# The prologue of an attention-plus-SwiGLU block on one core: the first token tile in two halves over two queues, its turned copy in two moves, and a shorter clear

## The chip, the cores and the metric

The kernel runs on one core of one Trainium2 chip. The time is that of one execution in microseconds (us); lower is better. Three runs of the kernel before gave 557.51, 557.83 and 559.01 us; the median is 557.83 us.

## What is computed

There are 2048 tokens of width 576. They are normalised (layernorm without gain or bias) and go through windowed causal attention (32 heads of width 18, window 256). A SwiGLU network with inner width 4608 runs on the same normalised tokens. The result is the sum of the tokens, the attention output and the network's output:

```
x = A_x
xn = _layernorm(x, axis=-1)
return x + _A_ref(xn, A_wqkv, A_wo) + _B_ref(xn, B_w1, B_w3, B_w2)
```

`_A_ref` projects to q, k and v, forms masked scores, takes a softmax, multiplies with v and projects with wo; `_B_ref` is `(silu(xn @ w1) * (xn @ w3)) @ w2`. All inputs are bf16.

## The kernel before

**Chunks.** The tokens go through in four chunks of 512 (loop at L959), each of four tiles of 128 tokens. A chunk has projections (`proj_part`, matmuls at L461), 36 SwiGLU units (matmuls at L713) with the attention scores woven in between (L587), and a second phase (L785) that multiplies with w2 and wo. Everything before L959 is the **prologue** of chunk 0: it loads the first four token tiles, normalises and turns them, and runs chunk 0's projections.

**How order and waits come about.** The program is a list of operations that is written out by hand. `add` (L59) appends an operation to its engine with the names of the buffers it reads (`r`), writes (`w`) or adds to (`j`); `resolve` (L90) turns these names into semaphore waits. Each engine runs its operations strictly in list order. A buffer name written once has one group of writers; every reader waits for all of them. DMAs are issued by SyncE (queue SPq) and by ScalarE (queue ACTq), in the order of their lists.

**The prologue in order.** The line numbers are those that the profile uses.

- L810 is ScalarE's table load and a small square root; L811 to L812 load the token tiles: tile 0 on SPq, tile 3 on ACTq, tile 1 on SPq, tile 2 on ACTq (`load_x`, DMA at L298, 128 rows of 576 elements each, into `xp`).
- L814 loads the first 512 rows of the v weights on SPq in two parts (`wv0`, `wv1`), L818 the last 64 rows on ACTq, once for each half of the partitions (`wvd`). L835 and L839 load the q and k weights on SPq.
- L821 clears `oq` on VectorE (256 f32 columns; later a buffer of the attention output). The cleared tile is the operand of **warming matmuls** (`warm`, L827): ten of 512 columns ahead of the first real work and one of 512 and one of 256 columns after the first turn. Their results are not used.
- Statistics: VectorE's `bn_stats` at L357 and L359 and `bn_aggr` at L360 for each tile. Tile 0 then gets its root on ScalarE (L362), a reciprocal (L382) and its normalised form `xn` (L386) with a small copy on GpSimd (L389). Tiles 1 and 2 get theirs through GpSimd (L365, L367) and VectorE (L371, L374). Tile 3 gets its sums on ScalarE (L860), a root (L876), a reciprocal (L882) and also L371 and L374.
- `xn_turn` (L399): ten transposes on TensorE (L406), five column blocks by two row halves, into two PSUM banks; then one move by ScalarE (L413) of 128x640 elements to `xnT`, the operand of all later matmuls.
- `proj_part` (L438) makes the matmuls of a projection in two parts: part 0 has ten (n from 0 to 4 by two row halves), part 1 has eight. For a v projection of tile i, matmul n reads column block n of `xnT` of that tile and the weights `wv0` (n of 0, 1), `wv1` (2, 3) or `wvd` (4).

TensorE's list in the prologue is: ten warming matmuls; turn of tile 0; two warming matmuls; v of tile 0, part 0; turn of tile 1; v of tile 0, part 1; turn of tile 2; v of tile 1, part 0; turn of tile 3; and then the rest of the projections. ScalarE's list is: root of tile 0; the sum over tile 3; the move of tile 0's turned copy; the sum of squares over tile 3; its root; the moves of tiles 1, 2 and 3.

Of the kernel before, what the change touches and what calls it, by code (L numbers as in the profile page):

```python
# [5 lines left out]
dt = mybir.dt  # L6
ACT = mybir.ActivationFunctionType
# [37 lines left out]
class _Prog:  # L45
# [13 lines left out]
    def add(self, eng, fn, r=(), w=(), j=(), dma=None, after=()):  # L59
        deps = []  # L60
        for k in r:
            deps += self.bufs[k].writers
        for k in w:
            g = self.bufs.get(k)
            if g is not None:
                deps += g.ahead(eng)
        for k in j:
            g = self.bufs[k].before
            if g is not None:
                deps += g.ahead(eng)  # L70
        op = _Op(eng, fn, deps + list(after), dma)
        op.after = tuple(after)
        self.n[eng] += 1
        op.pos = self.n[eng]
        if dma is not None:
            self.dma_count[dma] = self.dma_count.get(dma, 0) + 16
            op.cnt = self.dma_count[dma]
        for k in r:
            self.bufs[k].readers.append(op)
        for k in w:  # L80
            self.bufs[k] = _Gen([op], self.bufs.get(k))
        for k in j:
# [82 lines left out]
def bass_parallel_sum__sliding_block__glu_gated_swiglu__prompt_kernel(  # L165
# [17 lines left out]
    CH = 512  # L183
    NC = S // CH
    TB = CH // 128
# [7 lines left out]
    x2 = A_x[0]  # L193
    out2 = out[0]
    P = _Prog(nc)
    add = P.add

    with ExitStack() as es:

        def sb(name, shape, dtype=dt.bfloat16):  # L200
            return es.enter_context(nc.sbuf_tensor(name, shape, dtype))
# [4 lines left out]
        xp = [sb(f"xp{i}", [128, D]) for i in range(NXP)]  # L206
# [74 lines left out]
        def half_bank(b):  # L281
            return PS[:, b, :].bitcast(dt.bfloat16)
# [9 lines left out]
        xp_ctr = 0  # L292
# [106 lines left out]
        def xn_turn(t, banks, eng="dve"):  # L399
            i = t % 2  # L400
            c, tt = divmod(t, TB)
            for k in range(5):
                for r in range(2):
                    r0 = 64 * r
                    bv = half_bank(banks[r])[:, 64 * k:64 * k + 64]
                    add("pe", lambda e, bv=bv, r0=r0, k=k: e.transpose(  # L406
                        bv, xn[i][r0:r0 + 64, k * 128:(k + 1) * 128], ident[r0:r0 + 64, r0:r0 + 64],
                        tile_position=(r0, 0)),
                        r=[("xn", i), "ident"] + ([("xnd", i)] if k == 4 else []), **{"j" if k else "w": [("ps", banks[r])]})
            both = PS[:, banks[0]:banks[0] + 2, :].bitcast(dt.bfloat16)  # L410
            src = both[:, :, 0:320].rearrange("p r (k f) -> p k r f", f=64)
            dst = xnT[:, c % 2, :, tt * 128:(tt + 1) * 128].rearrange("p k (r f) -> p k r f", f=64)
            move = (lambda e: e.tensor_copy(dst, src)) if eng == "dve" else (lambda e: e.activation(dst, src, ACT.Copy))  # L413
            add(eng, move, r=[("ps", b) for b in banks], w=[("xnT", c % 2, tt)])

        def xn_send(t):
            i = t % 2
# [10 lines left out]
                    r=xk(c), dma=f"xnS{n}", **{"j" if n else "w": ["xnS"]})  # L428

        def xk(c):  # L430
            return [("xnT", c % 2, tt) for tt in range(TB)]


        def pair_of(c, i):

            return (((0, 1), (2, 3), (8, 4), (5, 6)) if c == 0 else ((8, 0), (1, 2), (3, 4), (5, 6)))[i]

        def proj_part(c, what, banks, part, behind=()):  # L438

            kind, i = what  # L440
            last = []
            for n in range(5 - part):
                for r in range(2):
                    x = r ^ part
                    kd, r0 = (4 if n == 4 else n), 64 * r
                    rows = slice(r0, r0 + 64)
                    out_ = PS[:, banks[x], :]
                    if kind == "q":
                        t = pair_of(c, i)[x]
                        st, mv = wp[rows, kd, t, :], xnT[rows, c % 2, kd, :]  # L450
                        keys = ["wpr" if n == 4 else "wp0"] + (["wp1"] if t > 3 else []) + (["wp8"] if t == 8 else []) + xk(c)
                    elif kind == "8":
                        out_ = PS[:, banks[x], 0:CH // 2]
                        st, mv = wp[rows, kd, i, :], xnT[rows, c % 2, kd, x * (CH // 2):(x + 1) * (CH // 2)]
                        keys = ["wpr", "wp0", "wp1"] + xk(c)
                    else:
                        out_ = PS[:, banks[x], 0:HD]
                        st, mv = xnT[rows, c % 2, kd, i * 128:(i + 1) * 128], wv[rows, kd, x * HD:(x + 1) * HD]
                        keys = ["wvd" if n == 4 else f"wv{n // 2}", ("xnT", c % 2, i)]
                    first = part == 0 and n == 0  # L460
                    op = add("pe", lambda e, out_=out_, st=st, mv=mv, n=n, r0=r0, first=first: e.matmul(  # L461
                        out_, st, mv, start=first, stop=(part == 1 and n == 3), tile_position=(r0, 0)),
                        r=keys, after=behind if n == 0 else (), **{"w" if first else "j": [("ps", banks[x])]})
                    if n == 4:
                        last.append(op)
            return last
# [188 lines left out]
        def o_scale(i):  # L655
            u3 = uqs[i].rearrange("p (n d) -> p n d", d=32)
            o3 = oq[:, :].rearrange("p (n d) -> p n d", d=32)[:, :, 0:Dh]
            add("dve", lambda e: e.reciprocal(rden[:], u3[:, :, Dh]), r=uq_keys[i], w=["rden"])
            add("pool", lambda e: e.tensor_tensor(  # L659
                o3, u3[:, :, 0:Dh], rden[:].unsqueeze(2).to_broadcast([128, CH // 32, Dh]), ALU.mult),  # L660
                r=uq_keys[i] + ["rden", "oq0"], w=["oq"])

        def o_turn(g, half):
            i = g // 2 % NOD
            c0 = half * (CH // 2)
            add("dve", lambda e: e.transpose(od[i][:, g % 2, c0:c0 + CH // 2], oq[:, c0:c0 + CH // 2]),  # L666
                r=["oq", "oq0"], **{"j" if half or g % 2 else "w": [("od", i)]})
# [140 lines left out]

        xslot = {}
        add("act", lambda e: e.activation(sm[:, 3:4], eps[:], ACT.Sqrt), r=["eps"], w=[("sm", 3)])  # L810
        for t in (0, 3, 1, 2):  # L811
            xslot[t] = load_x(t, "act" if t > 1 else "sp")  # L812
        for n in range(2):
            add("sp", lambda e, n=n: e.dma_start(  # L814
                wv[:, 2 * n:2 * n + 2, :], A_wqkv[256 * n:256 * n + 256, 2 * D:3 * D].rearrange("(kd p) f -> p kd f", p=128)),
                w=[f"wv{n}"], dma=f"wv{n}")
        for p in range(2):
            add("act", lambda e, p=p: e.dma_start(  # L818
                wv[64 * p:64 * p + 64, 4, p * HD:(p + 1) * HD], A_wqkv[512:576, 2 * D + p * HD:2 * D + (p + 1) * HD]),
                dma="wvd", **{"j" if p else "w": ["wvd"]})  # L820
        add("dve", lambda e: e.memset(oq[:].bitcast(dt.float32), 0.0), w=["oq0"])  # L821

        add("dve", lambda e: e.memset(qv[:, 0:2, :].bitcast(dt.float32), 0.0), w=[("q", g) for g in range(2)])

        def warm(b, *widths):
            for k, w in enumerate(widths):
                add("pe", lambda e, w=w: e.matmul(PS[:, b, 0:w], oq[:, 0:128], oq[:, 0:w], start=True, stop=True),  # L827
                    r=["oq0"], **{"j" if k else "w": [("ps", b)]})

        warm(4, *[CH] * 10)  # L830

        for h in range(2):
            for n in range(2):
                c0 = n * D + h * HD
                add("sp", lambda e, c0=c0: e.dma_start(  # L835
                    wa[:, 0:4, c0:c0 + HD], A_wqkv[0:512, c0:c0 + HD].rearrange("(kd p) f -> p kd f", p=128)),
                    dma=f"wqk{h}", **{"j" if n else "w": [f"wqk{h}"]})
# [32 lines left out]
        def turn(i):  # L870
# [6 lines left out]
            r=[("sm", 2), "eps"], w=[("sm", 3)])  # L877
# [23 lines left out]
        for h in range(2):  # L901
            a, b = 4 * h, 4 * h + 4
# [56 lines left out]
        for c in range(NC):  # L959
# [12 lines left out]
            start = 60 if c == 0 else 42  # L972
# [71 lines left out]
            for u in range(NF):  # L1044
# [7 lines left out]
                for n in range(9):  # L1052
                    into = nxt - (clock + 9 - n)
                    if (u, n) == JOINT[c]:
# [21 lines left out]
                        g = 2 * ja  # L1076
# [36 lines left out]
                if u in stat:  # L1113
                    t = (c + 1) * TB + stat[u]
# [4 lines left out]
                if u in apply:  # L1119
                    t = (c + 1) * TB + apply[u]  # L1120
# [6 lines left out]
                if c == 0 and u == 13:  # L1127
                    for t in range(4):
# [19 lines left out]
            banks = tail_bank = job()  # L1148
# [6 lines left out]
            for n, item in enumerate(p2_list(c)):  # L1155
# [20 lines left out]
                elif n in (100, 120) and c + 2 < NC:  # L1176
                    t = (c + 2) * TB + (n == 120)
# [32 lines left out]
```

## Time and profile before

| what | value |
|---|---|
| median of three runs | 557.83 us (557.51 to 559.01) |
| the profiled execution's own time | 557.61 us |
| its span, first to last instruction | 555.9 us |
| TensorE busy with matmuls | 552.1 us, 99% |
| VectorE, ScalarE, GpSimd busy | 56%, 47%, 29% |
| mean DMA rate | 155 GB/s |

All figures below are from this one profiled execution, whose time is 1.7 us longer than its span. A timeline row gives the start, the duration, the engine, the line, the operation and the tiles, and in brackets how long the engine had been idle before it and what ended that. PE is TensorE's matmuls and PEld its weight loads; the letter q after an engine's name marks its queue, that is, the issuing of a DMA. Matmuls overlap: one has a duration that includes its way through the array, while the next may start long before that ends.

### The profile page before, as it was taken

How to read it: one execution, taken by the hardware profiler on the slowest of the kernel's cores; microseconds unless marked ns; L12 is line 12 of the kernel's file. 1: busy time of each engine (PE TensorE's matmuls, PEld its weight loads, DVE VectorE, ACT ScalarE, POOL GpSimd, SP SyncE). 2: the span in 40 equal slices, each digit the busy share in tenths (PEclk: the TensorE clock that was granted, in tenths of full speed). 3: DMA queues.
4: the chain of work that ended last, by engine and by line, in shares of the span. 5: the costliest groups of instructions: out<-in, count | busy, mean ns of one | idle time of the engine just before them, and what ended most of it. 6: DMA issues, size and time to landing. Idle time of an engine off the chain costs nothing.

```text
span 555.9 us, 15754 instructions
## 1 busy us (share of the span) xinstructions
PE 552.1 (99%) x6772; PEld 346.6 (62%) x6772; DVE 311.4 (56%) x583; ACT 260.0 (47%) x359; POOL 162.7 (29%) x385
## 2 busy tenths in 40 slices
PE   8999999999999999999999999999999999999998
PEld 4666554677665545477766544847776554455776
DVE  6566978610365888851056687874105577678211
ACT  6457766100387774700048787550005777756000
POOL 5424534300034452530003454333001334333000
PEclk9999999999999999999999999999999999999999
DMA  9995989577377469756826748485582674553552
GB/s 244 201 206 139 211 188 243 106 196 186 90 143 164 114 138 167 217 136 174 203 57 140 169 126 198 123 205 136 151 187 54 138 174 122 150 151 82 142 150 65
DMA packets 127217, 85.96 MB, mean 155 GB/s; under 512 B 34452, under 2 KB 124908, under 8 KB 127148
## 3 DMA queue, kind: packets, MB, share of 16 engines
q1 hardware_dynamic: 125523, 83.49, 64.1%
q10 hardware_dynamic: 1624, 1.47, 1.0%
q8 instruction: 53, 0.87, 0.7%
q14 instruction: 17, 0.13, 0.1%
HBM read 71.29 MB, written 2.36 MB: 133 GB/s over the span
## 4 chain that ended last, share of the span: by engine, by line
PE 99%; ACT 0%; DVE 0%; issue 0%
PE ps L713 50%; PE ps L785 25%; PE ps L461 10%; PE ps L587 6%; PE ps L644 3%; PE ps L792 3%; PE ps L827 1%; PE ps L699 0%; PE ps L406 0%; ACT xnT L413 0%; DVE ofin L803 0%; DVE oq L821 0%
## 5 line engine op out<-in xcount | busy, mean ns | idle before, releaser
L713 PE MATMUL ps<-xnT,w 64*128 64x512 bf16 x1400 | 185.4, 376 | 0.0
L713 PE MATMUL ps<-xnS,w 64*128 64x512 bf16 x1120 | 154.0, 376 | 0.0
L785 PE MATMUL ps<-w,hT 128*128 128x288 bf16 x1156 | 146.7, 286 | 0.0
L728 DVE SCALAR_TENSOR_TENSOR gs<-th,ps 128x512 bf16<-128x512 bf16 x144 | 97.8, 679 | 76.6 <-ACT th L722 75.8
L785 PEld LDWEIGHTS ps<-w,hT 128*128 128x128 bf16 x1156 | 112.5, 98 | 28.9 <-issue 0.4
L713 PEld LDWEIGHTS ps<-xnT,w 64*128 64x128 bf16 x1400 | 73.0, 94 | 60.0 <-DVE ofin L653 0.2
L722 ACT ACTIVATE th<-ps 128x512 bf16<-128x512 f32 x144 | 85.6, 594 | 44.4 <-PE ps L713 42.0
L731 DVE SCALAR_TENSOR_TENSOR hT<-gs,ps 128x512 bf16<-128x512 bf16 x144 | 98.9, 687 | 4.9
L713 PEld LDWEIGHTS ps<-xnS,w 64*128 64x128 bf16 x1120 | 58.1, 94 | 46.7
L596 ACT ACTIVATE pt<-ps 128x1024 bf16<-128x1024 f32 (+1 forms) x70 | 70.8, 1011 | 31.2 <-PE ps L587 30.9
L474 ACT ACTIVATE stage<-ps 128x512 bf16<-128x512 f32 x16 | 9.5, 596 | 142.0 <-PE ps L461 142.0
L803 DVE TENSOR_TENSOR ofin<-ps,xp 128x288 bf16<-128x288 f32 x31 | 13.4, 455 | 108.3 <-PE ps L699 58.1
L623 POOL TENSOR_TENSOR hT<-hT,mk 128x128 int32<-128x128 int32 (+1 forms) x59 | 24.0, 429 | 170.5 <-ACT hT L596 170.3
L623 POOL TENSOR_TENSOR pt<-pt,mk 128x128 int32<-128x128 int32 (+1 forms) x124 | 49.9, 427 | 28.8 <-ACT pt L596 28.8
L587 PE MATMUL ps<-qv,kv 64*128 64x320 bf16 (+4 forms) x528 | 52.8, 260 | 0.0
L587 PEld LDWEIGHTS ps<-qv,kv 64*128 64x128 bf16 x528 | 27.4, 94 | 26.2 <-ACT hT L596 1.5
L596 ACT ACTIVATE w<-ps 128x1024 bf16<-128x1024 f32 (+1 forms) x32 | 32.3, 1010 | 12.3 <-PE ps L587 12.2
L461 PE MATMUL ps<-xnT,wp 64*128 64x512 bf16 (+1 forms) x360 | 38.0, 355 | 0.0
L596 ACT ACTIVATE hT<-ps 128x1024 bf16<-128x1024 f32 (+1 forms) x32 | 32.3, 1010 | 5.3 <-PE ps L587 4.8
L623 POOL TENSOR_TENSOR w<-w,mk 128x128 int32<-128x128 int32 (+1 forms) x56 | 22.9, 429 | 28.8 <-ACT w L596 28.8
L666 DVE STREAM_TRANSPOSE od<-oq 128x256 bf16<-128x256 bf16 x64 | 25.8, 427 | 6.9 <-POOL oq L659 6.9
L461 PEld LDWEIGHTS ps<-xnT,wp 64*128 64x128 bf16 x360 | 19.0, 94 | 14.4 <-ACT stage L474 0.2
(93 smaller groups left out, 384.9 us busy)
## 6 DMA issues: line engine op xcount, KB each, us to landing
w<-in_B_w_dram SPq DMA_DIRECT2D x210, 192.0 KB, 3.9
w<-in_B_w_dram SPq DMA_DIRECT2D x72, 288.0 KB, 3.3
xp<-in_A_x_dram SPq DMA_DIRECT2D x30, 144.0 KB, 4.5
out_dram<-ofin SPq DMA_DIRECT2D x31, 72.0 KB, 1.7
xnS<-xnT SPq DMA_DIRECT2D x8, 256.0 KB, 4.2
oT<-od SPq DMA_DIRECT2D x40, 36.0 KB
pt<-in_A_wqkv_dram SPq DMA_DIRECT2D x4, 288.0 KB, 6.0
hT<-in_B_w_dram SPq DMA_DIRECT2D x6, 192.0 KB, 5.2
```

The source lines that it names most:

```text
L461: op = add("pe", lambda e, out_=out_, st=st, mv=mv, n=n, r0=r0, first=first: e.matmul(out_, st, mv, start=first, stop=(part == 1 and n == ...
L587: add("pe", lambda e, r0=r0, out_=out_, kb=kb, q0=q0, nb=nb: e.matmul(out_, kb4[r0:r0 + 64, g, kb + NV - NB, :] if kb < 0 else kv[r0:r0 + ...
L596: add("act", lambda e: e.activation(pt_slot(sl)[:, 0:w, :], PS[:, SC[0]:SC[1] + 1, 0:w].rearrange("p r q -> p q r"), ACT.Exp, scale=scale) ...
L623: add("pool", lambda e, vb=vb, mm=mm: e.tensor_tensor(vb, vb, mm, ALU.mult), r=(key if n == 0 else []) + ["mk"], **{"w" if n == 0 else "j" ...
L644: add("pe", lambda e, p=p, q=q, pr=pr, sl=sl, g=g, pos=pos, q0=q0, nb=nb, col=col, first=first, n=n: e.matmul(PS[32 * q:32 * q + VW, banks ...
L666: add("dve", lambda e: e.transpose(od[i][:, g % 2, c0:c0 + CH // 2], oq[:, c0:c0 + CH // 2]), r=["oq", "oq0"], **{"j" if half or g % 2 els ...
L713: op = add("pe", lambda e, n=n, r0=r0, r=r, k=k, src=src: e.matmul(PS[:, b0 + r, :], wt[r0:r0 + 64, k, fl * 128:(fl + 1) * 128], src, star ...
L722: add("act", lambda e: e.activation(th[i][:], PS[:, bg, :], ACT.Tanh, scale=0.5), r=[("ps", bg)], w=[("th", i)])
L728: add("dve", lambda e: e.scalar_tensor_tensor(out=gs[i][:], in0=th[i][:], scalar=1.0, in1=PS[:, bg, :], op0=ALU.add, op1=ALU.mult), r=[("t ...
L731: add("dve", lambda e: e.scalar_tensor_tensor(out=hT[:, u, :], in0=gs[i][:], scalar=0.5, in1=PS[:, bu, :], op0=ALU.mult, op1=ALU.mult), r= ...
L785: add("pe", lambda e: e.matmul(bank, hT[:, f, tt * 128:(tt + 1) * 128], w2[sl][:, k, n0:n1], start=first, stop=(c + 1 == NC and half == 1 ...
L792: add("pe", lambda e: e.matmul(bank, oT[:, k, tt * 128:(tt + 1) * 128], wo[:, k, d0 + n0:d0 + n1], start=False, stop=(k == 3 and (half == ...
```

## The change

Four edits, all in the prologue.

1. Token tile 0 is no longer loaded by one DMA on SPq. Rows 0 to 63 are loaded on SPq and rows 64 to 127 on ACTq, both ahead of all other loads. Tiles 3, 1 and 2 follow on the queues that they had.
2. The clear of `oq` becomes two instructions with names of their own, `oq0` for the first 64 f32 columns (128 bf16 columns) and `oq1` for the other 192. Both stand ahead of the loads in the list. The warming matmuls read only the first 128 bf16 columns, repeated by a broadcast. The later users of `oq` (L659, L666) name both parts.
3. The first run of warming matmuls is nine of 512 columns and one of 256 in place of ten of 512.
4. The move of tile 0's turned copy is two ScalarE instructions, of column blocks 0 to 1 and of 2 to 4. The second has the name `xnT0`, and only those matmuls of tile 0's v projection with n over 1, and all users of the whole chunk, wait for it.

```
-            add(eng, move, r=[("ps", b) for b in banks], w=[("xnT", c % 2, tt)])
+            for n, (k0, k1) in enumerate(((0, 2), (2, 5)) if t == 0 else ((0, 5),)):
+                src = both[:, :, 64 * k0:64 * k1].rearrange("p r (k f) -> p k r f", f=64)
+                dst = xnT[:, c % 2, k0:k1, tt * 128:(tt + 1) * 128].rearrange("p k (r f) -> p k r f", f=64)
...
+                add(eng, move, r=[("ps", b) for b in banks], w=["xnT0" if n else ("xnT", c % 2, tt)])
...
         def xk(c):
-            return [("xnT", c % 2, tt) for tt in range(TB)]
+            return [("xnT", c % 2, tt) for tt in range(TB)] + (["xnT0"] if c == 0 else [])
...
-                        keys = ["wvd" if n == 4 else f"wv{n // 2}", ("xnT", c % 2, i)]
+                        keys = ["wvd" if n == 4 else f"wv{n // 2}", ("xnT", c % 2, i)] + (["xnT0"] if c + i == 0 and n > 1 else [])
...
-        for t in (0, 3, 1, 2):
+        for n, (c0, c1) in enumerate(((0, 64), (64, CH // 2))):
+            add("dve", lambda e, c0=c0, c1=c1: e.memset(oq[:].bitcast(dt.float32)[:, c0:c1], 0.0), w=[f"oq{n}"])
+        for p, eng in enumerate(("sp", "act")):
+            add(eng, lambda e, p=p: e.dma_start(xp[0][64 * p:64 * p + 64, :], x2[64 * p:64 * p + 64, :]),
+                dma="xp0", **{"j" if p else "w": [("xp", 0)]})
+        xslot[0], xp_ctr = 0, 1
+        for t in (3, 1, 2):
             xslot[t] = load_x(t, "act" if t > 1 else "sp")
...
-        add("dve", lambda e: e.memset(oq[:].bitcast(dt.float32), 0.0), w=["oq0"])
...
-                add("pe", lambda e, w=w: e.matmul(PS[:, b, 0:w], oq[:, 0:128], oq[:, 0:w], start=True, stop=True),
+                add("pe", lambda e, w=w: e.matmul(PS[:, b, 0:w], oq[:, 0:128], oq[:, 0:128].unsqueeze(1).to_broadcast([128, w // 128, 128]), start=True, stop=True),
...
-        warm(4, *[CH] * 10)
+        warm(4, *[CH] * 9, 256)
```

On the queues the first issues become: SPq tile 0 upper half, tile 1, `wv0`, `wv1`, then the q and k weights; ACTq tile 0 lower half, tile 3, tile 2, the two `wvd`.

More of the change, by code (lines that the diff above doesn't have):

```diff
@@ L410, in xn_turn @@
             both = PS[:, banks[0]:banks[0] + 2, :].bitcast(dt.bfloat16)
-            src = both[:, :, 0:320].rearrange("p r (k f) -> p k r f", f=64)
-            dst = xnT[:, c % 2, :, tt * 128:(tt + 1) * 128].rearrange("p k (r f) -> p k r f", f=64)
-            move = (lambda e: e.tensor_copy(dst, src)) if eng == "dve" else (lambda e: e.activation(dst, src, ACT.Copy))
-            add(eng, move, r=[("ps", b) for b in banks], w=[("xnT", c % 2, tt)])
+            for n, (k0, k1) in enumerate(((0, 2), (2, 5)) if t == 0 else ((0, 5),)):
+                src = both[:, :, 64 * k0:64 * k1].rearrange("p r (k f) -> p k r f", f=64)
+                dst = xnT[:, c % 2, k0:k1, tt * 128:(tt + 1) * 128].rearrange("p k (r f) -> p k r f", f=64)
+                move = (lambda e, dst=dst, src=src: e.tensor_copy(dst, src)) if eng == "dve" else (
+                    lambda e, dst=dst, src=src: e.activation(dst, src, ACT.Copy))
+                add(eng, move, r=[("ps", b) for b in banks], w=["xnT0" if n else ("xnT", c % 2, tt)])
         def xn_send(t):
@@ L660, in o_scale @@
                 o3, u3[:, :, 0:Dh], rden[:].unsqueeze(2).to_broadcast([128, CH // 32, Dh]), ALU.mult),
-                r=uq_keys[i] + ["rden", "oq0"], w=["oq"])
+                r=uq_keys[i] + ["rden", "oq0", "oq1"], w=["oq"])
         def o_turn(g, half):
@@ L666, in o_turn @@
             add("dve", lambda e: e.transpose(od[i][:, g % 2, c0:c0 + CH // 2], oq[:, c0:c0 + CH // 2]),
-                r=["oq", "oq0"], **{"j" if half or g % 2 else "w": [("od", i)]})
+                r=["oq", "oq0", "oq1"], **{"j" if half or g % 2 else "w": [("od", i)]})
         def o_move(eng, dst, src, key, first, sem, r):
```

## The prediction

> **What bounds the kernel now.** First the page's part 1, which says whether any engine but TensorE can matter at all; then the chain that ended last and the timeline, for the first 12 us alone.
>
> ```profile
> PE 552.1 (99%) x6772; PEld 346.6 (62%) x6772; DVE 311.4 (56%) x583; ACT 260.0 (47%) x359; POOL 162.7 (29%) x385
> ```
>
> TensorE is busy for 552.1 of 555.9 us. The change touches only what stands ahead of the first chunk, so it can do one thing: let TensorE's unbroken work begin sooner or later. Everything behind moves with that. The chain in the prologue:
>
> ```profile
> 1.24 4.45 PE ps L827 x10
> ...
> 6.23 0.71 ACT xnT L413
> ...
> 7.08 0.79 PE ps L461 x10
> 7.87 0.22 PE ps L406 x10
> 8.09 0.50 PE ps L461 x8
> ...
> 8.61 0.43 PE ps L406 x10
> ```
>
> Read alone, this says: ten warming matmuls, turn, ScalarE's move, projection. Each edit shortens one of these links. But matmuls overlap, and the chain follows an engine through its own pipeline; it can't see that TensorE could have begun earlier. The timeline's brackets can:
>
> ```profile
> 3.55 0.46 DVE L357 BATCH_NORM_STATS2 stats<-xp 128x6 f32<-128x288 bf16 x1 [1.82 <-DMA xp<-in_A_x_dram]
> 5.17 0.43 DVE L386 TENSOR_SCALAR xn<-xp,mv,rstd 128x576 bf16<-128x576 bf16 x1
> 5.65 0.40 PEld L406 LDWEIGHTS ps<-ident,xn 64*128 64x128 bf16 x10 [0.87 <-DVE xn L386]
> 6.93 0.21 DVE L360 BATCH_NORM_AGGREGATE mv<-stats 128x2 f32<-128x12 f32 x1
> 7.53 0.57 POOL L367 TENSOR_TENSOR rstd<-vpe,neghalf 128x1 f32<-128x1 f32 x1
> 8.14 0.41 DVE L371 TENSOR_SCALAR xn<-xp,mv,rstd 128x512 bf16<-128x512 bf16 x1 [0.31 <-POOL rstd L367]
> 8.60 0.32 PEld L406 LDWEIGHTS ps<-ident,xn 64*128 64x128 bf16 x10 [0.32 <-DVE xn L371]
> ```
>
> Both turns wait for VectorE: tile 0's (5.65) for `xn` of L386, which ends at 5.60, and tile 2's (8.60) for `xn` of L371, which ends at 8.55. VectorE begins at 3.55, as tile 0 lands, and has almost no gap after that; its last wait is for GpSimd's root of tile 2 (7.53+0.57 = 8.10), which hangs on VectorE's aggregate at 6.93. So the real chain up to 8.6 us is: tile 0 lands, VectorE's list, tile 2's turn. TensorE has slack there: the eight matmuls of 8.09 span 0.50 with a drawn-out last one of 0.28 (the row of L461 below), so the array takes the next work from about 8.4, 0.2 us before `xn` is there.
>
> **Part by part.**
>
> *The shorter clear and the shorter warming.*
>
> ```profile
> 0.91 0.27 DVE L821 MEMSET oq<- 128x256 f32 x1 [0.91 <-PEq L1195]
> 1.24 0.48 DVE L823 MEMSET qv<- 128x512 f32 x1
> L827 PE MATMUL ps<-oq x12: 414/631/631, 1.2 to 6.5; 128*128 128x512 bf16 x11, 128*128 128x256 bf16 x1
> ```
>
> Two clears give 0.21 us for 256 columns more, so 64 columns take 0.27 - 192 x 0.00083 = 0.11 and warming starts at 1.08 in place of 1.24. Ten matmuls take 4.45 of which the last one's 0.63 is drawn out, so one per (4.45-0.63)/9 = 0.424. The array is through with ten at 1.24+4.24 = 5.48, and the turn waits until 5.65 for `xn`: this link isn't the last wait by 0.17. After the change: 1.08 + 9.5 x 0.424 = 5.11. The 0.37 is worth something only if `xn` comes sooner; cost and gain at nothing, hidden by tile 0's statistics. The second clear (192 columns, some 0.2 us) lies in the 1.82 us in which VectorE waits. I take the repeated 128 columns at the price of 512 plain ones; no row shows a broadcast operand, and up to 0.5 us over the ten it is covered, below nothing there is no reason.
>
> *The move in two.*
>
> ```profile
> 6.23 0.70 ACT L413 ACTIVATE xnT<-ps 128x640 bf16<-128x640 bf16 x1 [0.63 <-PE ps L406]
> L474 ACT ACTIVATE stage<-ps 128x512 bf16<-128x512 f32 x16 | 9.5, 596 | 142.0 <-PE ps L461 142.0
> 6.83 0.77 ACT L860 ACTIVATE stage<-xp,sm 128x576 bf16<-128x576 bf16 x1
> 7.52 0.31 DVE L374 TENSOR_SCALAR xn<-xp,mv,rstd 128x128 bf16<-128x128 bf16 x1
> 7.72 0.29 ACT L876 ACTIVATE sm<-sm,eps 128x1 f32<-128x1 f32 x1
> 8.69 0.15 DVE L882 RECIPROCAL sm<-sm 128x1 f32<-128x1 f32 x1
> L461 PE MATMUL ps<-wv,xnT x72: 279/283/293, 7.1 to 13.4; 64*128 64x288 bf16 x72
> ```
>
> 640 against 512 elements is 0.704 against 0.596, so 0.00084 per element: the parts take 0.38 and 0.49. The first ends at 6.61 instead of 6.93, and v of tile 0 can start 0.32 sooner, behind the two warming matmuls, about 6.8. The second ends near 7.0 (ScalarE takes the next 0.1 ahead of an end: 6.23+0.70 against 6.83), so n over 1 runs from about 7.15 and part 0 ends 0.2 sooner. It then meets tile 1's turn, whose last column block waits for L374 (7.52+0.31 = 7.83), just when TensorE comes to it now. So the 0.2 ends in a wait for VectorE there, and again at 8.60. Worth: nothing while tile 0 lands when it does. ScalarE's sum of squares starts 0.07 later (0.38+0.49-0.1 against 0.70); the root behind it is ready at 8.0 and VectorE wants it at 8.69: covered by 0.6.
>
> *Tile 0 over two queues.* This alone can move the chain.
>
> ```profile
> 0.79 0.88 SPq L298 DMA_DIRECT2D xp<-in_A_x_dram  x2
> 0.93 0.88 ACTq L298 DMA_DIRECT2D xp<-in_A_x_dram  x2
> L298 SPq DMA_DIRECT2D xp<-in_A_x_dram x2: 402/410/417, 0.8 to 1.2; - x2
> L818 ACTq DMA_DIRECT2D wv<-in_A_wqkv_dram x2: 562/586/609, 1.8 to 2.4; - x2
> xp<-in_A_x_dram SPq DMA_DIRECT2D x1, 144.0 KB, 2.7
> xp<-in_A_x_dram ACTq DMA_DIRECT2D x1, 144.0 KB, 3.0
> 2.00:2.25 0.25, 0.25 (x2) 0.15 (x1) 0.00 (x0) 0.24 (x2) 0.23 (x1) 1.00 1.35 152
> 2.75:3.00 0.25, 0.25 (x2) 0.07 (x1) 0.00 (x0) 0.00 (x0) 0.25 (x2) 1.00 1.07 350
> ```
>
> (The last two rows end in DMA GB/s.) Tile 0 lands at 0.79+2.7 = 3.5, tile 3, the first on ACTq, at 0.93+3.0 = 3.9. Against the split: a DMA of 64 rows (L818) takes 0.56 to 0.61 to issue, one of 128 rows 0.40. So SPq's half is issued by 1.38 instead of 1.19, ACTq's by 1.52. For it: half the bytes per queue. At 350 GB/s 72 KB take 0.2; at the start, where the rate is 152, 0.5. Early bound: ACTq's half behaves like SPq's: 0.93 + 2.7 + 0.19 of issue - 0.5 = 3.3. Late bound: it behaves like tile 3, which needed 0.3 more for the same issue time: 0.93+3.0+0.19-0.2 = 3.9. The late end takes half the bytes at the fast rate; at the slow rate, as in the early one, it is 3.6. Between 3.3, 3.6 and 3.9 I take 3.5, the value of tile 0's own row: what the shorter transfer saves, the longer issue and the second queue's later start take back. Both ends go into the range: 0.2 less, 0.4 more.
>
> The Trainium skill ("DMA: Bandwidth & Descriptors", section "Why a DMA increments its semaphore by 16 and not by 1") says that a queue's DMA spreads over the largest number of engines up to 16 that divides its rows, the lowest-numbered ones; 64 rows and 128 rows both get the same 16. By that a second queue adds no engine, and the sum stays as it is; if the halves had engines of their own, 0.2 more would be saved. No row of this trace names a packet's engine.
>
> *What the loads move.*
>
> ```profile
> xp<-in_A_x_dram SPq DMA_DIRECT2D x1, 144.0 KB, 3.1
> 4.53 0.41 DVE L357 BATCH_NORM_STATS2 stats<-xp 128x6 f32<-128x288 bf16 x1
> 4.84 0.67 ACT L860 ACTIVATE stage<-xp 128x576 bf16<-128x576 bf16 x1
> ```
>
> Tile 1, next on SPq, is issued at 0.79+0.44 = 1.23 and lands 3.1 later, at 4.3; it is wanted at 4.53. It goes behind half a tile less on its queue, so I see no new wait. ACTq's tile 3, tile 2 and `wvd` are issued about 0.6 later. Tile 3 lands at 3.9 and is wanted at 4.84, 0.9 in hand; tile 2 stands behind both other tiles' statistics on VectorE and has more. `wvd` has less; that is a rival.
>
> **Sum.** 557.61 (profiled execution) + 0 = 557.6. That execution lies 0.2 under the median of 557.83, which the range covers.
>
> **Rivals.**
>
> *Both halves flow early.* Tile 0 lands at 3.3. Everything on VectorE's list moves up by 0.2, the shorter warming (5.11) and the split move are then in time, and tile 2's turn starts at 8.4: 557.4. For it: the rate of 152 GB/s around 2 us, far under 350, is room that a second queue could fill. Against: the longer issue.
>
> *`wvd` takes the place (slower).*
>
> ```profile
> wv<-in_A_wqkv_dram ACTq DMA_DIRECT2D x1, 36.0 KB, 4.6
> ```
>
> The second `wvd` (issued at 2.4 by L818's row) lands at 2.4+4.6 = 7.0. Its users are the last two of the ten matmuls of v of tile 0 (n of 4), at 7.08 + 0.79 - 0.28 = about 7.55 now. On TensorE tile 1's turn is queued behind them, then part 1 of v and tile 2's turn. If `wvd` lands as much later as it is issued (0.6), it is there at 7.6 and costs next to nothing; it decides from about 7.8, where TensorE's 0.2 of slack at 8.6 is used up. Landing behind the q weights too (another 0.4, 8.0) costs 0.2 to 0.4: 557.8 to 558.0. The late landing of tile 0 (3.9) gives the same end. Against: the queue's own backlog only grows by half a tile, 0.2 at 350 GB/s.
>
> *TensorE's pace doubles later.*
>
> ```profile
> 6.12 0.82 PE L827 MATMUL ps<-oq 128*128 128x512 bf16 x2
> ```
>
> Up to 6.1 TensorE takes 0.424 for 512 columns; from 7.08 (the chain's row of ten) five pairs of matmuls of 288 columns take 0.79-0.28 = 0.51, or about 0.12 each: twice the pace. Somewhere between, the pace doubles, after work without gaps except 0.17 ahead of the first turn. The change widens this gap to 5.65-5.11 = 0.54 if tile 0 lands as now, and narrows the one before 7.08. If the doubling takes a stretch without such a gap and starts over, TensorE stays slow past 7.08. As long again as from 1.24 to 7.08 after 5.65 is 11.5: half of 4.4 is lost, 2.2 us, 559.8 at most. The Trainium skill ("TensorE: Matmul & The Clock Gate", section "Part 1: The HAM clock gate") has the gate decide by busy windows of 3.4 us that run freely, so a missed one costs one window: an estimate of half of 3.4 less some waits, 1.3 us, 558.9. The trace shows the doubling, not the window; the page's clock column reads 1.00 from the start.
>
> **How the numbers follow.** No change within 0.1 of 557.6: 0.47. Early: 0.25. Late `wvd` or late tile 0: 0.16. Late pace: 0.10, of which 0.04 over 559.3. Another 0.02 for something faster that I don't see. Range 557.1 to 558.9: below the early case by the spread of runs (0.3), up to the missed window. By 0.3% (1.7 us), about what a measurement of this kernel can tell from no change: faster 0.02, same 0.93, slower 0.05.
>
> **What would show it.** Landing: L357's bracket ends between 3.4 and 3.6 on the forecast; 3.3 says early. The weight loads of tile 0's turn still wait for L386, longer than 0.87. L461's first ten start near 6.8 and end sooner, tile 1's and tile 2's turns wait for L374 and L371 as long as was won. If L461 waits for a DMA instead, the `wvd` rival holds; if its ten take over 1 us, the pace does. Wrong would be a gain with tile 0 landing at 3.5.

## The result, and the profile after

| | before | after |
|---|---|---|
| median (lowest to highest), us | 557.78 (557.48 to 559.01), 6 runs | 560.38 (559.23 to 560.94), 6 runs |
| ratio over the compared runs, 95% interval (not the quotient of the medians) | | 1.0040 (1.0027 to 1.0054) |
| profiled execution: time, span, us | 557.61, 555.9 | 560.57, 558.9 |
| first q projection starts, us | 11.96 | 14.91 |

The change makes the kernel slower: by 2.6 us in the medians, by 2.2 (1.5 to 3.0) by the ratio, and by 2.96 in the two profiled executions. The forecast was no change, 557.6 with a range of 557.1 to 558.9; the new median lies 1.5 above the end of that range.

The whole difference is made ahead of one point. The first group of q projection matmuls (`ps<-xnT,wp` x10) is the first work that comes after all of chunk 0's turning; it starts 2.95 later, and the time is 2.96 longer. This start, "the q projection starts at", is the gauge used below. The chain of waits of after, its first 30 us (start, length, what):

```profile
1.56 0.73 ACTq L298
2.32 0.45 ACTq L298
2.81 0.56 ACTq L826
3.40 5.43 DMA wv<-in_A_wqkv_dram
8.83 0.05 issue
8.88 0.42 PE ps L463
9.30 0.27 PE ps L406 x7
```

Before, the same chain ran through warming, turn, move and projection. Now it runs through ScalarE's DMA queue: three issues one behind the other, then the second `wvd` load (L826), issued at 3.40 and landed 5.43 later, at 8.83. TensorE goes on from there. The timeline of after on TensorE (start, length, engine, operation, and in the bracket the idle time ahead and what ended it):

```profile
1.04 4.23 PE L833 MATMUL ps<-oq 128*128 128x512 bf16 x10 [1.04 <-DVE oq L814]
5.83 0.53 PE L406 MATMUL ps<-ident,xn 64*128 64x64 bf16 x10 [0.55 <-DVE xn L386]
6.29 0.82 PE L833 MATMUL ps<-oq 128*128 128x512 bf16 x2
7.05 1.14 PE L463 MATMUL ps<-wv,xnT 64*128 64x288 bf16 x8
8.88 0.42 PE L463 MATMUL ps<-wv,xnT 64*128 64x288 bf16 x2 [0.69 <-DMA wv<-in_A_wqkv_dram]
...
12.07 3.00 PE L463 MATMUL ps<-wv,xnT 64*128 64x288 bf16 x36
14.91 1.24 PE L463 MATMUL ps<-xnT,wp 64*128 64x512 bf16 x10
```

The same two rows at the end, of before:

```profile
9.74 2.38 PE L461 MATMUL ps<-wv,xnT 64*128 64x288 bf16 x36
11.96 1.24 PE L461 MATMUL ps<-xnT,wp 64*128 64x512 bf16 x10
```

Two losses are to be seen. The ten matmuls of tile 0's v projection are torn in two: the pair that reads `wvd` waits 0.69. And the pace: eight matmuls take 1.14 where before ten took 0.79, and the group of 36 takes 3.00 where it took 2.38; TensorE does the early v work at half pace until about 13.4. Before, the pace had doubled ahead of 7.08. If the same matmuls are laid side by side in both traces, after is 0.17 behind at the first turn, 0.03 ahead at the first v matmul, 0.28 behind at the last of the eight, 1.41 at tile 1's turn, 1.71 at tile 2's, and 2.96 at the 93rd matmul; from there it stays. From tile 1's turn on no row of TensorE has a wait, so the last 1.55 of the 2.96 is made at half pace, without a wait.

VectorE's and ScalarE's timelines of after, the rows that answer to those of the landings and of the split move:

```profile
3.71 0.46 DVE L357 BATCH_NORM_STATS2 stats<-xp 128x6 f32<-128x288 bf16 x1 [1.98 <-DMA xp<-in_A_x_dram]
6.92 0.46 DVE L357 BATCH_NORM_STATS2 stats<-xp 128x6 f32<-128x288 bf16 x1 [0.54 <-DMA xp<-in_A_x_dram]
9.03 0.41 DVE L371 TENSOR_SCALAR xn<-xp,mv,rstd 128x512 bf16<-128x512 bf16 x1 [0.55 <-POOL rstd L367]
```

```profile
6.40 0.77 ACT L415 ACTIVATE xnT<-ps 128x256 bf16<-128x256 bf16 x2 [0.63 <-PE ps L406]
```

VectorE starts on tile 0 at 3.71 (3.55 before) and then waits 0.54 for tile 2, which it never did before. The move in two takes 0.77.

The issues on the two queues, of after (start, length, queue):

```profile
0.79 0.61 SPq L816 DMA_DIRECT2D xp<-in_A_x_dram  x1
1.46 0.56 SPq L298 DMA_DIRECT2D xp<-in_A_x_dram  x1
2.06 0.95 SPq L822 DMA_DIRECT2D wv<-in_A_wqkv_dram  x2
3.05 1.15 SPq L841 DMA_DIRECT2D pt<-in_A_wqkv_dram  x2
0.93 0.60 ACTq L816 DMA_DIRECT2D xp<-in_A_x_dram  x1
1.56 0.74 ACTq L298 DMA_DIRECT2D xp<-in_A_x_dram  x1
2.32 0.45 ACTq L298 DMA_DIRECT2D xp<-in_A_x_dram  x1
2.81 1.21 ACTq L826 DMA_DIRECT2D wv<-in_A_wqkv_dram  x2
```

and the two that matter, of before:

```profile
2.70 1.18 SPq L835 DMA_DIRECT2D pt<-in_A_wqkv_dram  x2
2.43 0.61 ACTq L818 DMA_DIRECT2D wv<-in_A_wqkv_dram  x1
```

Before, the second `wvd` was issued 0.27 ahead of the first load of q weights (288 KB, tile `pt`). After, it is issued at 3.40 and the q weights at 3.05: the order has turned round. The times from issue to landing, put together from the rows of DMA issues of both traces:

| load | before: issue, landing | after: issue, landing |
|---|---|---|
| tile 0 | SP 0.79, 3.52 | SP 0.79, 3.05 and ACT 0.93, 3.69 |
| tile 1 | SP 1.25, 4.34 | SP 1.46, 4.15 |
| tile 3 | ACT 0.93, 3.92 | ACT 1.56, 4.94 |
| tile 2 | ACT 1.35, 4.74 | ACT 2.32, 6.89 |
| `wv0`, `wv1` | SP 1.71, 5.85; 2.19, 6.76 | SP 2.06, 5.99; 2.54, 7.38 |
| `wvd`, first and second | ACT 1.83, 5.69; 2.43, 6.99 | ACT 2.81, 7.36; 3.40, 8.83 |
| first q weights | SP 2.70, 7.76 | SP 3.05, 8.55 |

Read by issue time, either half of the table gives landings in the same order, whichever queue a load is on, but for pairs that land within 0.2 of each other. In that order `wvd` has fallen back by one load of 288 KB. The order is not strict in the other traces: there a small load often lands ahead of a 288 KB load that was issued before it, by 0.41 in `a_whole`, by 0.98 in `b_short`, and by 1.37 in `a_wvd_sp`, where both are on SPq. The second `wvd` keeps to it closely: issued at 2.43, ahead of the q weights, it landed at 6.59, 6.99 and 7.54 in three kernels; issued at 3.3 to 3.4, behind them, at 8.47 to 8.96 in five. For tile 0 itself nothing was gained: its second half lands at 3.69.

### The profile page after: what moved, and what is told of

Read it like the earlier page. It is cut to its first block, busy times and chain, and to the rows that moved or that the text cites. A ratio compares the mean times of both kernels' runs of the same rounds, so it can differ in the third digit from the quotient of the medians.

```text
span 558.9 us, 15758 instructions
## 1 busy us (share of the span) xinstructions
PE 554.1 (99%) x6772; PEld 336.2 (60%) x6772; DVE 310.9 (56%) x584; ACT 260.0 (47%) x360; POOL 162.8 (29%) x385
## 3 DMA queue, kind: packets, MB, share of 16 engines
q10 hardware_dynamic: 1704, 1.55, 1.0%
## 4 chain that ended last, share of the span: by engine, by line
PE 98%; DMA 1%; ACTq 0%; ACT 0%; DVE 0%; issue 0%
PE ps L715 50%; PE ps L787 25%; PE ps L463 10%; PE ps L589 6%; PE ps L646 3%; PE ps L794 3%; DMA wv<-in_A_wqkv_dram 1%; PE ps L701 0%; ACTq L298 0%; PE ps L406 0%; ACT L812 0%; ACTq L826 0%; DVE ofin L805 0%
## 5 line engine op out<-in xcount | busy, mean ns | idle before, releaser
L715 PEld LDWEIGHTS ps<-xnT,w 64*128 64x128 bf16 x1400 | 68.7, 94 | 64.2 <-DVE ofin L655 0.2
L715 PEld LDWEIGHTS ps<-xnS,w 64*128 64x128 bf16 x1120 | 54.6, 94 | 50.0
L805 DVE TENSOR_TENSOR ofin<-ps,xp 128x288 bf16<-128x288 f32 x31 | 13.4, 455 | 108.3 <-PE ps L701 58.1
L589 PEld LDWEIGHTS ps<-qv,kv 64*128 64x128 bf16 x528 | 25.9, 94 | 27.7 <-ACT hT L598 1.5
```

Of the source, the lines that this page charges most:

```text
L589: add("pe", lambda e, r0=r0, out_=out_, kb=kb, q0=q0, nb=nb: e.matmul(out_, kb4[r0:r0 + 64, g, kb + NV - NB, :] if kb < 0 else kv[r0:r0 + ...
L715: op = add("pe", lambda e, n=n, r0=r0, r=r, k=k, src=src: e.matmul(PS[:, b0 + r, :], wt[r0:r0 + 64, k, fl * 128:(fl + 1) * 128], src, star ...
```

## Theories

**Late `wvd`** (the prediction's slow rival, larger): splitting tile 0 makes the issues longer, the second `wvd` drops behind the q weights, TensorE waits. **Late pace** (the other rival): warming that ends sooner and a first turn that begins no sooner leave a gap; TensorE stays at half pace. **Edits 2 to 4**: the shorter clear, the shorter warming or the split move cost something by themselves.

## Experiments

### Which of the four edits

`a_whole`: all of after, but tile 0 whole on SPq.

```
-        for p, eng in enumerate(("sp", "act")):
-            add(eng, lambda e, p=p: e.dma_start(xp[0][64 * p:64 * p + 64, :], x2[64 * p:64 * p + 64, :]),
-                dma="xp0", **{"j" if p else "w": [("xp", 0)]})
-        xslot[0], xp_ctr = 0, 1
-        for t in (3, 1, 2):
+        for t in (0, 3, 1, 2):
```

> The changed kernel with tile 0 in one DMA on SPq again; the shorter clear, the shorter warming and the move in two stay. Queue theory (half of tile 0 on ACTq pushes wvd and tile 2 back, TensorE waits for wvd, all else follows): the 2.6 us are gone, 557.3 to 558.0, wvd lands near 7.0, no matmul of L461's group waits for a DMA. Warming theory (the wider gap ahead of the first turn keeps TensorE at half pace, with or without the queues): the gap is still about 0.5 us, so 559 or more.

Measured 557.98 against 557.64, 0.9998 (0.9988 to 1.0008). The q projection starts at 11.83, 0.13 before that of before. No matmul's row has a wait for a DMA; one weight load waits 0.33 for `wv1`, which landed at 7.00. The gap of 0.55 ahead of the first turn is there; the pace had doubled before it.

`b_split`: before with the split of tile 0 alone (the reverse of the diff above).

> The kernel before with tile 0 in two halves over both queues, and nothing else of the change. Queue theory: as slow as the changed kernel, 559.8 to 560.9, wvd landing at 8.5 to 9. Warming theory: only the wait itself, about 0.9 us, since the warming is as long as before: 558.3 to 558.9, TensorE at full pace by 7.

Measured 559.65 against 557.64, 1.0029 (1.0018 to 1.0040), between the two forecasts; `wvd` lands at 8.96 as the one has it, the pace is full by 7 as the other has it. The q projection starts at 13.31. In the TensorE timeline and the chain of this kernel:

```profile
9.01 0.30 PE L461 MATMUL ps<-wv,xnT 64*128 64x288 bf16 x2 [0.92 <-DMA wv<-in_A_wqkv_dram]
```

```profile
3.41 5.55 DMA wv<-in_A_wqkv_dram
```

The split alone brings the wait for `wvd` and most of the loss, with ten whole warming matmuls ahead and the pace doubled (the pair takes 0.30, not 0.42). Edits 2 to 4 by themselves (`a_whole`) are worth nothing that can be measured. The third theory falls.

### Is it `wvd`, and what stands behind it

`a_light`: after, with tiles 1, 3, 2 all on SPq, so that ACTq carries only tile 0's lower half and `wvd`.

```
-        for t in (3, 1, 2):
-            xslot[t] = load_x(t, "act" if t > 1 else "sp")
+        for t in (1, 3, 2):
+            xslot[t] = load_x(t)
```

> The changed kernel with tiles 1, 3 and 2 all on SPq behind tile 0's half, so that wvd stands right behind tile 0's other half on ACTq. The halves stay. Queue theory: wvd lands before 6.5 and tile 2 before 6, no wait for a DMA behind tile 0: 557.3 to 558.2. If the two halves themselves (64 rows each, tile 0 landing at 3.6 to 3.7) are the cost: 558.5 or more.

Measured 558.27 against 557.67, 1.0015 (1.0005 to 1.0025), just over the forecast of the queue theory, which had no wait for a DMA. `wvd` is issued at 2.33 and there at 5.18, and no pair waits for it. But its place is taken:

```profile
7.82 0.54 PE L463 MATMUL ps<-wv,xnT 64*128 64x288 bf16 x6 [0.42 <-DMA wv<-in_A_wqkv_dram]
```

Four matmuls wait 0.28 for `wv0` (landed at 6.94), and the next six wait for `wv1`, issued at 3.75 behind three tiles and landed at 7.78. The q projection starts at 12.38: 0.42 late in place of 2.95. Most of the loss goes with the late `wvd`; the rest is the longer row of issues, which makes some other load late.

`a_order`: tile 0 whole again, tiles 0, 3, 2 on SPq, tile 1 and `wvd` on ACTq; the short clear and the split move stay, with ten warming matmuls.

```
...
+        for t in (0, 1, 3, 2):
+            xslot[t] = load_x(t, "act" if t == 1 else "sp")
...
-        warm(4, *[CH] * 9, 256)
+        warm(4, *[CH] * 10)
```

> Tile 0 whole on SPq, then tiles 3 and 2 there; ACTq carries tile 1 and wvd alone; the shorter clear and the move in two stay, ten warming matmuls of 512. Queue theory: wvd lands near 5.5, nothing waits for it in any run: 557.2 to 557.7, at or a little under the kernel before. Else 558 or more.

Measured 557.79 against 557.67, 1.0000 (0.9990 to 1.0009). `wvd` is there at 5.49 and nothing waits for it; six matmuls wait 0.20 for `wv1` (landed at 7.14). The q projection starts at 11.75, 0.21 earlier than before, yet the span of this execution is 556.5, longer than before's 555.9: TensorE stood 0.56 at one place near 224 us (last section). A gain of 0.2 can't be told from no change here. No version tried beat the kernel before.

`a_wvd_sp`: after, with `wvd` on SPq behind `wv1`, ahead of the q weights (`add("sp", ...)` in place of `add("act", ...)`).

> The changed kernel with the two wvd DMAs on SPq behind wv1 instead of on ACTq. Queue theory, wvd alone: no wait of 0.7 us any more, tile 2 still late (landing near 6.9), which leaves some 0.5 us: 557.8 to 558.6. Queue theory with tile 2 as important: 558.6 to 559.5. Warming theory: 559 or more, with the pace doubling after 9.

Measured 558.93 against 557.64, 1.0017 (1.0003 to 1.0031). This was meant as a cure. In its profiled execution, the slowest of the ten, every load was late (tile 2 at 7.70, `wv1` at 8.49, `wvd`, issued at 3.59, at 9.18), so it says little on what `wvd` costs; it says more on the pace, below. Its five runs at a granted clock of 1.000 (table below) have a median of 558.09, 0.45 over the kernel before, so in those most of the loss is gone.

`b_late`: before, with `wvd` alone made late, on SPq behind the first two loads of q and k weights; tile 0 whole.

> The kernel before with one thing late: the two wvd DMAs stand on SPq behind the first two q and k weight loads, and tile 0 stays whole. Tile 2 then comes as early as before. If the late wvd is the whole price of the split: 558.8 to 559.8, like the split alone. If tile 2's lateness (VectorE's list) carries most of it: 557.6 to 558.4.

Measured 560.81 against 557.67, 1.0053 (1.0036 to 1.0070), a microsecond over the higher forecast. `wvd` lands at 9.79, later than in after.

```profile
9.84 0.30 PE L461 MATMUL ps<-wv,xnT 64*128 64x288 bf16 x2 [2.20 <-DMA wv<-in_A_wqkv_dram]
```

A late `wvd` is enough by itself to make the kernel slower, with tile 0 as it was. The q projection starts 3.60 later: 2.2 of wait and, behind it, half pace (below).

`a_wvd_first`: after, with `wvd` right behind tile 0's lower half on ACTq, ahead of tiles 3 and 2.

> The changed kernel with wvd on ACTq right behind tile 0's lower half, ahead of tiles 3 and 2, which are then issued still later than in the changed kernel. wvd lands before 6. If wvd alone carries the loss: 557.6 to 558.3. If tile 2, now later than 7, takes over as what VectorE's list and tile 2's turn wait for: 558.4 to 559.2, and L357's last pair waits for its DMA by a microsecond or more.

Measured 562.63 against 557.91, 1.0081 (1.0063 to 1.0099), the worst of all and far over the forecast, though what was to wait did wait. `wvd` is there at 6.18, but tile 2 is issued at 3.63, behind the q weights:

```profile
xp<-in_A_x_dram ACTq DMA_DIRECT2D x1, 144.0 KB, 6.0
```

It lands at 9.66, and VectorE and then TensorE wait for it:

```profile
9.68 0.46 DVE L357 BATCH_NORM_STATS2 stats<-xp 128x6 f32<-128x288 bf16 x1 [3.22 <-DMA xp<-in_A_x_dram]
```

```profile
11.08 0.46 PE L406 MATMUL ps<-ident,xn 64*128 64x64 bf16 x10 [1.69 <-DVE xn L371]
```

ACTq's two late loads can't both go first: whichever is last falls behind the q weights.

### Is it the q weights that pass ahead

`a_qk_wait` and `a_qk_hold`: after, with the loads of the q and k weights held until tile 0, or until tile 3 (the second in its buffer), has landed.

```
-                    dma=f"wqk{h}", **{"j" if n else "w": [f"wqk{h}"]})
+                    r=[("xp", 1)], dma=f"wqk{h}", **{"j" if n else "w": [f"wqk{h}"]})
```

(`a_qk_wait` has `("xp", 0)` there.)

> The changed kernel with one more wait: SPq issues the q and k weights only when tile 0 has landed, about 3.6 us, some 0.6 us later than it does. ACTq is untouched, its wvd is issued as late as in the changed kernel. If transfers land in the order in which both queues issue them (the q and k weights stand ahead of wvd only because SPq issues them first), wvd lands near 7.3 and the time falls to 557.8 to 558.8. If ACTq is late by its own backlog and the halves' longer issue, wvd still lands at 8.5 or later: 559.8 to 560.8.

Measured 559.39 against 557.91, 1.0026 (1.0016 to 1.0035). The edit was too weak: the q weights are issued at 3.30 instead of 3.05, still 0.02 ahead of the second `wvd`, which lands at 8.79, as late as in after. So it doesn't test the order, but gives a second kernel with after's loads.

> The changed kernel with the q and k weights held on SPq until tile 3 has landed (about 4.9 us), so that SPq surely issues them behind both wvd; waiting for tile 0 moved them by only 0.25 us, to 0.03 us ahead of the second wvd. If transfers land in the order of issue over both queues: the second wvd lands behind wv1, at 7.3 to 7.9 instead of 8.8, TensorE's matmuls of n = 4 start there, and the time is 558.2 to 559.0. If wvd is late for a reason of ACTq's own: it lands at 8.5 or later, 559.3 to 560.6.

Measured 558.80 against 557.78, 1.0013 (1.0004 to 1.0023), inside the forecast of the common order. The q weights are issued at 4.99, and the second `wvd`, issued at 3.34, lands at 7.99. Against after's 8.83 one 288 KB load passing ahead costs it 0.8 us; against the 8.47 to 8.96 of the five kernels in which it passes, 0.5 to 1.0. The other 1.0 of its 1.84 comes with its own later issue and the loads that still stand ahead. The time doesn't come back with it, since the next loads are as late. Its TensorE timeline:

```profile
7.79 0.54 PE L463 MATMUL ps<-wv,xnT 64*128 64x288 bf16 x6 [0.52 <-DMA wv<-in_A_wqkv_dram]
8.63 0.43 PE L406 MATMUL ps<-ident,xn 64*128 64x64 bf16 x10 [0.29 <-DVE xn L371]
...
9.81 0.42 PE L406 MATMUL ps<-ident,xn 64*128 64x64 bf16 x10 [0.27 <-DVE xn L371]
```

First `wv1` (7.75), then VectorE's lists of tile 1 and of tile 2 (landed at 7.21). The q projection starts at 13.13, as in `a_qk_wait` (13.15). In after, tile 2's lateness lies hidden beside the wait for `wvd`.

### What the pace adds

`b_short`: before, with six warming matmuls instead of ten (`warm(4, *[CH] * 6)`); all loads as before.

> The kernel before with six warming matmuls of 512 columns in place of ten: a gap of about 1.8 us ahead of the first turn, loads as before. Warming theory: the pace doubles one stretch of 3.4 us later than before, 1.2 to 2.2 us lost: 559 to 560. Queue theory without a part for the gap: 557.5 to 558.

Measured 558.53 against 557.64, 1.0005 (0.9994 to 1.0017): unclear as a time, and in neither forecast. The profiled execution, the slowest of the ten, had more idle time than the shorter warming makes: `wv0` and `wv1` landed at 6.84 and 7.83, and TensorE waited 0.46 and 0.48 for them. Its stretches show the pace (stretch, length, busy time of PE, PEld, DVE, ACT, POOL, granted clock, DMA share, GB/s):

```profile
4.50:7.80 3.30, 1.34 (x16) 0.52 (x16) 3.06 (x10) 2.56 (x7) 1.79 (x6) 1.00 1.04 323
7.90:11.30 3.40, 3.40 (x46) 2.30 (x48) 2.27 (x7) 1.42 (x3) 0.93 (x3) 0.50 1.09 228
11.40:14.00 2.60, 2.60 (x52) 1.99 (x48) 0.98 (x3) 2.26 (x6) 1.25 (x6) 1.00 1.06 232
```

After 3.3 us with TensorE busy for 1.34 the granted clock falls to 0.50 for 3.4 us, and is 1.00 again behind it. `b_late` shows the same behind its wait:

```profile
7.40:10.80 3.40, 1.20 (x32) 0.81 (x30) 1.47 (x7) 0.95 (x4) 0.57 (x1) 1.00 1.13 245
10.90:14.20 3.30, 3.30 (x43) 2.11 (x39) 1.51 (x4) 2.22 (x6) 3.03 (x9) 0.50 0.59 155
```

and `a_wvd_sp` too:

```profile
5.80:9.10 3.30, 1.69 (x20) 0.53 (x20) 1.79 (x7) 1.87 (x6) 1.39 (x5) 1.00 1.13 314
9.20:12.50 3.30, 3.27 (x52) 2.36 (x54) 2.35 (x8) 1.41 (x2) 1.72 (x4) 0.50 1.06 221
```

The Trainium skill ("TensorE: Matmul & The Clock Gate", section "Part 1: The HAM clock gate") has a clock gate that judges activity by free-running windows of 3.4 us and is therefore different from run to run. The traces agree with that length: in each of these three the clock is at 0.50 for 3.4 us in one piece, in `b_short` from 7.89 to 11.31.

Not every early wait costs the pace. In `a_qk_wait`, with three waits of 0.26 to 0.87, TensorE is busy for 2.13 of 3.41 from 3.86 to 7.27 and for 2.20 of 3.42 from 7.27 to 10.69, and the clock stays at 1.00. When the pace first doubles also differs from execution to execution. The trace's record of the granted clock begins at that moment: at 6.80 in before, at 13.38 in after, and between 3.86 and 6.54 in ten of the twelve experiments (two have no such record). In `a_whole` and `b_split` it came at 4.54 and 4.56, still in the warming, so their gap of 0.55 ahead of the first turn could not delay it. In `a_wvd_first` it came at 6.20, behind a gap of 0.63.

`a_warm11` and `a_fill`: after with eleven whole warming matmuls, which close the gap ahead of the first turn; `a_fill` moreover with two discarded matmuls of 512 columns ahead of the pair that waits for `wvd`.

```
-        warm(4, *[CH] * 9, 256)
+        warm(4, *[CH] * 11)
...
+                if kind == "v" and c + i + part == 0 and n == 4:
+                    warm(3, CH, CH)
```

> The changed kernel with eleven warming matmuls of 512 columns ahead of the first turn in place of nine and a half, so that TensorE doesn't stand still before it; no filler at the wait for wvd. If the gap ahead of the first turn is what keeps the pace at half in the changed kernel: as with both fillers, 558.6 to 559.3. If the wait for wvd does it as well: 559.5 to 560.5.

> The changed kernel with filler: eleven warming matmuls of 512 columns ahead of the first turn, and two more right ahead of the two matmuls that wait for wvd. The loads are as late as in the changed kernel, TensorE has more to do and stands still less. If half pace, brought on by standing still, is a part of the loss: 558.3 to 559.3, with full pace from about 6 to 10 on. If only the waits for wvd and tile 2 count: 560 to 561.

`a_warm11`: 559.28 against 557.91, 1.0035 (1.0021 to 1.0049). `a_fill`: 558.95 against 557.67, 1.0026 (1.0017 to 1.0035). Both lie inside the forecast that has the pace as a part of the loss, `a_warm11` at its edge. In the profiled executions the pace is full from 5.5 (`a_warm11`) and 4.0 (`a_fill`), and the wait remains, here in `a_warm11`:

```profile
8.52 0.30 PE L463 MATMUL ps<-wv,xnT 64*128 64x288 bf16 x2 [0.70 <-DMA wv<-in_A_wqkv_dram]
```

The q projection starts at 12.83 and 13.13, later than before by 0.87 and 1.17; in `b_split` and `a_qk_wait`, also at full pace, it is 1.35 and 1.19. That is the wait without the pace; after's 2.95 holds 1.6 to 2.1 more. But the intervals of these kernels overlap with after's, so the medians alone don't separate the two. The granted clock of each single run does, in part: it was 1.000 or 0.997 in nearly all, and 0.997 is what one stretch of 3.4 us at 0.50 makes of 557 us (1 - 0.5 x 3.4 / 557). It is 0.994 in three of `a_wvd_first`'s four runs, two such stretches.

| kernel | runs at 0.997 or less | median at 1.000 | median at 0.997 or less |
|---|---|---|---|
| before, all that ran beside the experiments | 1 of 88 | 557.78 | 559.91 |
| a_whole, a_order | 0 of 20 | 557.98, 557.79 | |
| after | 3 of 6 | 560.57 | 560.24 |
| a_warm11 | 4 of 10 | 559.06 | 561.33 |
| a_qk_wait | 4 of 10 | 559.07 | 559.83 |
| a_wvd_sp | 5 of 10 | 558.09 | 559.64 |
| b_split | 3 of 10 | 559.15 | 560.00 |
| a_light | 2 of 10 | 558.10 | 559.82 |
| b_short | 2 of 10 | 558.38 | 559.20 |
| a_fill | 1 of 10 | 558.87 | 560.98 |
| a_qk_hold | 1 of 10 | 558.77 | 559.53 |
| a_wvd_first | 3 of 4 | 561.77 | 563.27 |
| b_late | 4 of 4 | | 560.81 |

With every load in time and enough warming the clock is nearly never taken back. With an early wait, or too little warming, it is in a part of the runs, and a run in which it is taken back is 0.8 to 2.3 us longer than the same kernel's others (after's alone are not). `a_warm11`, `a_qk_wait` and `a_fill` at 1.000 lie 1.15, 1.16 and 1.20 over the median of the kernel before beside which they ran, and `b_split` 1.51: the cost of the late loads without a clock taken back. The rest of after's loss, 0.7 to 1.4 of 2.2 to 2.6, is the pace on this reckoning. The clock column doesn't show a doubling that merely comes late: after's profiled execution reads 1.000 and still ran the v projection at half pace. That may be why its 1.000 runs are no faster; the other two of them have no trace.

## Why the prediction was wrong

**"ACTq's tile 3, tile 2 and `wvd` are issued about 0.6 later"**, and **"the queue's own backlog only grows by half a tile, 0.2 at 350 GB/s"**: these are the steps that failed. The second `wvd` was issued 0.97 later, since not one issue became longer but several: 0.60 for the half tile, and 0.74 for the whole tile behind it (0.44 before, half of 0.88). And the backlog was counted on its own queue, while in before and after the loads land in one order over both. 0.97 carried it past the q weights: landing 1.84 later, not 0.6. "Landing behind the q weights too" was foreseen and given 0.4; it cost 0.8 (0.5 to 1.0).

**The `wvd` rival** had the right mechanism and the right users: what it foretold for L461 waiting on a DMA is what the timeline shows. Its threshold of 7.8 was not tested. Its size was wrong (8.0, it was 8.83), so its 0.2 to 0.4 was 1.2 to 1.5. The start times of both queues side by side would have shown the turn-round with the prediction's own numbers: 2.43 + 0.6 = 3.03 for the second `wvd` against 2.70 + 0.19 = 2.89 for the q weights, so landing behind them was the case to expect and not the exception. Its chance of 0.16 was too small for that.

**"tile 2 ... has more"**: it had 1.39 in hand (4.74 against VectorE's row at 6.13), but it was 2.15 late (6.89), and VectorE waited 0.54 for it. Where `wvd` comes sooner (`a_qk_hold`, `a_wvd_first`) it sets the end; in after it is hidden by `wvd`.

**The pace rival** had the right effect. The gap ahead of the first turn came out at 0.55 (forecast 0.54), and the half pace lasted until 13.4 (forecast 11.5). Its price of 1.3 to 2.2 was about right (1.55 behind the wait, in the profiled execution). That the gap is what kept the pace down is not shown: `a_wvd_first` has a wider one, 0.63, and doubled at 6.20. And it was treated as a separate case of 0.10, but the two rivals aren't separate: a wait for a load is itself idle time that can cost the pace (`b_late`). Together they make the loss that was measured, which no case of the forecast had.

**"I take 3.5"** for tile 0 held roughly: 3.69, inside its two ends of 3.3 and 3.9. Over the kernels with the split the later half landed between 3.29 and 3.80, the whole tile between 3.31 and 3.52. The Trainium skill ("DMA: Bandwidth & Descriptors", section "Rules for kernel authors") says of two transfers to separate halves of the partitions that they share the same engines and one whole transfer is better. The traces agree as far as the landing goes: no pair of halves was complete clearly sooner than a whole tile. The early rival falls.

**The edits at nothing held.** Warming starts at 1.04 (1.08), and ten matmuls with a repeated operand take 4.23: no extra price. The two moves of ScalarE take 0.77 together; without the split of tile 0 (`a_whole`) edits 2 to 4 come out at 0.13 at the q projection and at nothing in the time. The links that were shortened indeed weren't the last waits.

What stays open: how much of the mean loss is the pace in after itself. Its share is 1.55 or more in the one execution that has a trace; the 0.7 to 1.4 is a difference between kernels, and no run had after's loads with a pace that could not be lost. Three kernels whose loads come as in after have ratios of 1.0040 (after), 1.0029 (`b_split`) and 1.0026 (`a_qk_wait`), with intervals that overlap.

## What to carry to other kernels

A load that is made longer at the head of a queue must be followed through to the last small load of that queue: write down the issue times of all queues in one list, and see which load is overtaken, since a 288 KB load that slipped ahead by 0.35 us delayed the small one here by about 0.8. A wait in the first microseconds is to be priced twice, as wait and as pace. And where several loads of a prologue are all just in time, mending one shows the next: here `wv1` (`a_light`) and tile 2 (`a_wvd_first`) took over from `wvd`.

## What the runs showed of the hardware

- Loads from SPq and ACTq land in the order in which they were issued on either, within 0.2 us, in before and after (table above). Other traces have small loads landing ahead of earlier 288 KB loads, by up to 1.4. Why is not settled: one common order, or two queues that share the engines evenly with like backlogs, would look alike here.
- A DMA of 64 rows takes longer to issue (0.60 and 0.61 in after) than one of 128 rows (0.40 and 0.42 in before), and the 128-row issue behind it is longer as well (0.56 and 0.74).
- The granted clock comes back to 0.50 for 3.4 us after a stretch in which TensorE was busy for 35 to 51% of the time (1.20 of 3.40, 1.69 of 3.30), with single gaps of no more than 2.2 us. It stays at 1.00 in `a_qk_wait`, where the two stretches are busy for 62 and 64%. Where between 51 and 62% it turns, if the share is what counts, no run here shows.
- In three executions TensorE stands once near 224 us with nothing that the profile shows to wait for: 0.56 in `a_order` (below), 0.31 in `a_warm11`, 0.14 in `a_qk_hold`. From the q projection to the end these take 0.3 to 0.8 us longer than before. Neither before nor after has it; its cause is open.

```profile
223.94 0.23 PE L589 MATMUL ps<-qv,kv 64*128 64x128 bf16 x2 [0.56 <-issue]
```
